# Windowed attention with a soft mixture of experts on one core: the attention stage looped over pairs of head groups instead of single groups

## Chip, cores and metric

One NeuronCore of a Trainium2 chip runs the whole program. The metric is the device time of one execution in microseconds (us), as the median of several runs. PE is the matrix engine (PEld its weight loads), DVE the vector engine, ACT the scalar engine, POOL the GpSimd engine, SP the engine whose queue issues nearly all DMA transfers. Each engine works through its own instructions in program order, and semaphores make it wait for others.

## What is computed

```python
# q, k, v: (8 batches, 8 heads, 576 positions, 64)
scores = (q @ k^T) / 8 + bias           # bias = -slope[head] * |i - j|
scores = where(0 <= i - j < 128, scores, -1e9)
attn   = exp(scores - max); attn /= sum + 1e-9
x      = (attn @ v) as (4608 tokens, 512)
logits = x @ phi                        # 8 experts x 4 slots = 32 columns
d = softmax of logits over all tokens;  c = softmax of logits over the 32 slots
slot_input = d^T @ x                    # (8, 4, 512)
slot_out   = relu(slot_input @ w1[e]) @ w2[e]
out        = c @ slot_out               # (4608, 512)
```

## The kernel before, in words

**Tiles and groups.** A batch has five query tiles: t = 0 to 3 with 128 queries and t = 4 with 64. A query sees 128 keys back, so a tile's keys lie in its own and the previous tile. The eight heads of a tile are done as two groups g = 0, 1 of four heads (tile 4 has one group for all eight). `groups` (line 150) lists all 72 groups (b, t, g); the last batch takes its tiles in the order 1, 2, 3, 4, 0.

**The steps of a group.**
- `scores` (225): matmuls into one of two score buffers `s4s[i % 2]` in PSUM: a bias by a ramp (L231, L243, bf16), then q times k (L236, L250). The array is split into tiles of 64 rows by 32 columns there.
- `softmax_front` (306), for the new group and the one before it (`old`): on DVE `merge` (L263 to L267) lays the two halves of the window over each other, `rowmax` (L281) takes the maximum, `inverse` (L293) the reciprocal of the old group's sums, `bias` (L284) the new group's scaled maximum, `normalise` (L298) multiplies the old group's four blocks by the reciprocals. Between merge and maximum in the program, `total` (L289) adds an epsilon to the old group's sums, on POOL. `filler` puts pending small DVE steps of the slot softmax between them.
- `expo` (327): four exps on ACT (L333) with their row sums; they read the score buffer and write P into one of three buffers `p4s`.
- `flip` (338): four transposes of P on PE (L343) into the PSUM bank `pt`; full 128x128 layout.
- `split` (345): ACT copies the flipped P to SBUF (L350); in tiles 1 to 3 two selects on POOL cut it into the part that belongs to the previous tile's keys (L352) and the part of the own tile's keys (L354); tile 4 has its own pair (L357, L359). Tile 0 has no previous keys and needs no select.
- `values` (364): P times v on PE (L380) into the PSUM bank `xp`, in tiles of 128 rows by 64 columns. Both selects must be done, since each pair of heads uses both parts.
- `x_store` (389): when both groups of a tile are done, ACT copies the result from `xp` (L396).

**What happens to x.** Per batch: `x_flip` (398, L401) transposes each tile into the bank `xq`, `x_keep` (409, L410) copies it on ACT; `logits` (415, L419; every second batch also the packed tail tiles, L430) multiply x by phi into the bank `mi`; `token_*`, `slot_*` and `slots_*` do a running softmax over tokens and one over slots, with small transposes (L458, L486), `slot_sum` (498, L502; with a tail L509) and an update of the accumulator on DVE (`slot_add`, L515).

**PSUM.** Eight banks: two score buffers of two banks each, and one bank each for `pt`, `xp`, `xq`, `mi`. A bank is written again only when its reader has finished.

**The order of work.** The order on each engine is the order of the program (`manual_schedule` over all five). The loop (773 to 800) runs over groups i: softmax front of group i, flip and split of group i - 3 (`FLAG`), values of group i - 4 (`LAG`), scores of group i + 1, loads, exps of group i. Steps on x are put into lists by `do` in `after_values` (726) and taken out by `run` at five places of an iteration. `load_weights_at` (716) issues weight loads in between, some 36 of them during attention. Behind the loop stand the last groups and the joining of the slot statistics, written out by hand (802 to 889), and then the experts and the output (891 on).

Of the kernel before, what the change touches and what calls it, by code (L numbers as in the profile page):

```python
# [21 lines left out]
DM = H * D  # L22
# [22 lines left out]
LAG = 4  # L45
# [22 lines left out]
def tile_attn_softmoe(  # L68
# [55 lines left out]
    place = [ks[1], areas[14], ks[0], ks[2]] + [areas[i] for i in (0, 10, 6, 4, 16, 12, 8)]  # L124
# [273 lines left out]
    def x_flip(b, t, to=None):  # L398
        xq = ps_1.tile([P, DM], F32, tag="xq", name="xq") if to is None else to
        for j in range(NPAIR):  # L400
            nc.tensor.transpose(xq[:, P * j:P * j + P], x_of(b, t)[:, j], ident)  # L401
        st["xq", b, t] = xq
# [95 lines left out]
    def slot_sum(b):  # L498
        dn = st["d", b]
        ap = ps_1.tile([P, DM], F32, tag="mi" if b < last else "pt", name="ap")  # L500
        for c in range(lanes(b)):
            nc.tensor.matmul(  # L502
                ap[NS * c:NS * c + NS], lhsT=dn[:, NS * c:NS * c + NS], rhs=xns[c],
                start=True, stop=(c < 3 or not with_tail(b)),
            )
        st["a", b] = ap
# [209 lines left out]
    def load_weights_at(i):  # L716
        b, t, g = groups[i]
        if i >= W0 and loaded[0] < NW and (NW - loaded[0]) * (WEND - W0 - 2) >= NW * (WEND - i):
            load_weight()
        if groups[i] == (last, 3, 1):  # L720
            load_v(True)
        if b == last and (t == 0 and g == 0 or t == 4):
            assert loaded[0] >= NW
            load_weight()

    def after_values(i, key):
        b, t, g = key
        if not (g == 1 or t == 4):
# [6 lines left out]
        x_store(b, t, nc.scalar)  # L735
        tail = with_tail(b)
        late = b > 0 and b % 2 == 0
        if p == 0 and late:
            do("mid", i + 3, x_flip, b, t)
            do("act", i + 4, x_keep, b, t)  # L740
        elif t < 4:
            do("pe", i + 1 + (p == 1 and late), x_flip, b, t)
            if b < last or p == 0:
                do("act", i + 2 + (p == 0 or p == 1 and late), x_keep, b, t)
        if p == (4 if b < last else 1):
            do("pe", i + 1, logits, b)
            if tail:
                do("pe", i + 1, logits_tail, b)
            if b == last:
                return  # L750
            do("act", i + 2, token_copy, b)
            do("dve", i + 2, token_max, b)
            do("pe", i + 2, slot_flip, b)
            do("act", i + 3, token_exp, b)
            do("dve", i + 3, token_sum, b)
            do("pe", i + 3, token_flip, b)
            do("act", i + 4, token_keep, b)
            do("pre", i + 4, slots_max, b)
            do("pe", i + 4, slot_sum, b)
            do("act", i + 5, slots_exp, b)  # L760
            if tail:
                do("pe", i + 2, x_flip, b, 4)
                do("pe", i + 4, x_keep, b, 4)
                do("pe", i + 5, slot_tail, b)
                do("dve", i + 5, slot_add, b)
            else:
                do("pre", i + 5, slot_add, b)
            do("dve", i + 6, later, slots_norm, b)

    with tc.manual_schedule(engines=ORDERED):  # L770
        scores(0)
        loads(0)
        for i in range(n):
            new = groups[i]
            run("pre", i)
# [28 lines left out]
        def bank(tag):  # L804
            return ps_1.tile([P, NPAIR, P], F32, tag=tag, name="bank")

        def quarters(x):
            return x.rearrange("p (u w) -> p u w", u=4)

        x_keep(last, 2)  # L810
        token_copy(last)
# [3 lines left out]
        slot_flip(last)  # L815
        token_max(last)
        values(ga)
        load_weight()
        load_weight()
# [3 lines left out]
        flip(gc, to=quarters(free[0]))  # L823
        split(gc)
        token_exp(last)
        total(gd, LO)
        inverse(gd, LO)
        normalise(gd, LO)
        values(gb, range(0, 2), bank("xq"))
        flip(gd, LO)  # L830
        split(gd, LO)
        total(gd, HI)
        inverse(gd, HI)
        normalise(gd, HI)
        values(gb, range(2, 4))
        load_weight()
        flip(gd, HI, quarters(free[2]))
        split(gd, HI)
        token_sum(last)
        x_store(last, 3)  # L840
# [47 lines left out]
        run("dve", n)  # L888
# [225 lines left out]
```

## Time and profile before

| | |
|---|---|
| median of 3 runs | 297.35 us (297.21 to 297.76) |
| profiled execution, own time | 297.64 us |
| its span, first to last instruction | 295.9 us |
| mean granted PE clock | 0.974 |
| PE busy / weight loads | 277.5 / 196.7 us |
| DVE, ACT, POOL busy | 240.8, 208.6, 93.2 us |
| attention loop | to about 220 us |

The timeline of a view gives the start of an instruction (or of a run of equal ones) in us from the span's start, its length, the engine, the line, what it writes and reads, its shape and the count; in brackets how long the engine stood idle before it and whose event ended that. A flip counts as four PE records, values of a group of tiles 1 to 3 as 16, scores as 8 of the bias and 32 of q times k. Matmuls overlap, and their ends are modelled, so distances between starts tell more than lengths. [...]

### The profile page before, as it was taken

To read this page: it belongs to the slowest core of one execution; us is meant where nothing else is said; L and a number is where in the kernel's file an instruction comes from. 1 tells how busy PE (TensorE), PEld (TensorE's weight loads), DVE (VectorE), ACT (ScalarE), POOL (GpSimd) and SP (SyncE) were. 2 spreads that over 40 slices of the span, in tenths; PEclk is the share of its full clock that TensorE was granted. 3 is DMA by queue.
4 is the path that set the end of the run, shared out by engine and by line. 5 is a ranking of instruction groups with operands and counts; after the bars stand their busy time and mean duration, and the time that the engine had idled before them with its cause. 6 is when DMAs were issued, how large, how long until landed. Compare 5 with 4: busy or idle time off the path is not lost. (4 is left out here: it accounts for less than half of the span.)

```text
span 295.9 us, 13063 instructions
## 1 busy us (share of the span) xinstructions
PE 277.5 (94%) x5131; PEld 196.7 (66%) x5131; DVE 240.8 (81%) x745; ACT 208.6 (70%) x814; POOL 93.2 (31%) x207
## 2 busy tenths in 40 slices
PE   5599999999999999999999999999898999999990
PEld 2367877777677777776777777667676653587650
DVE  2899999998989999988999998979897345646451
ACT  3688888977988988977888977978686331035460
POOL 2025525442444254244415442445454011000000
PEclk9579999999999999999999999999999999999996
DMA  6545268878686878867688877857357489999897
GB/s 203 187 130 174 78 200 255 274 234 259 200 255 219 259 245 276 265 204 249 207 275 260 278 233 240 255 182 234 110 167 281 144 292 327 411 409 342 336 384 278
DMA packets 36753, 72.58 MB, mean 245 GB/s; under 512 B 4402, under 2 KB 15316, under 8 KB 36692
## 3 DMA queue, kind: packets, MB, share of 16 engines
q1 hardware_dynamic: 35972, 71.24, 72.7%
q8 instruction: 40, 0.66, 0.9%
q10 hardware_dynamic: 720, 0.51, 0.5%
q14 instruction: 21, 0.17, 0.2%
HBM read 62.29 MB, written 9.44 MB: 242 GB/s over the span
## 5 line engine op out<-in xcount | busy, mean ns | idle before, releaser
L333 ACT ACTIVATE area<-s,nb 128x128 f32<-128x128 f32 x288 | 102.7, 377 | 17.3 <-DVE nb L284 13.0
L380 PE MATMUL xp<-area 128*64 128x128 f32 (+1 forms) x1104 | 78.1, 273 | 1.7 <-DMA area<-v_n 0.9
L298 DVE TENSOR_SCALAR area<-area,rs 128x128 f32<-128x128 f32 x286 | 79.0, 337 | 0.4
L380 PEld LDWEIGHTS xp<-area 128*64 128x64 f32 (+1 forms) x1104 | 58.1, 136 | 17.7 <-issue 9.9
L333 ACT ACTIVATION_READ_ACCUMULATOR area<-s,nb 128x1 f32 x288 | 61.8, 214 | 0.0
L281 DVE TENSOR_REDUCE s<-s 128x4 f32<-128x512 f32 (+1 forms) x73 | 50.4, 690 | 2.3
L350 ACT COPY area<-pt 128x512 f32<-128x512 f32 (+1 forms) x72 | 42.3, 590 | 13.3 <-PE pt L343 12.2
L289 POOL TENSOR_SCALAR rs<-sm 128x4 f32<-128x4 f32 x70 | 14.1, 202 | 100.8 <-ACT area L333 100.0
L343 PE MATMUL pt<-unit_r,area 128*128 128x128 f32 x282 | 45.4, 284 | 0.0
L250 PE MATMUL s<-kq 64*32 64x160 f32 x1792 | 42.6, 305 | 0.0
L343 PEld LDWEIGHTS pt<-unit_r,area 128*128 128x128 f32 x282 | 31.8, 143 | 14.1 <-PE s L250 5.0
L352 POOL TENSOR_SCALAR_AFFINE_SELECT area<-area 128x512 f32<-128x512 f32 x48 | 31.3, 651 | 27.1 <-ACT area L350 25.4
L265 DVE COPY_PREDICATED s<-cst,s 128x512 f32<-128x512 int32 x48 | 33.0, 686 | 1.0 <-PE s L250 0.8
L354 POOL TENSOR_SCALAR_AFFINE_SELECT area<-area 128x512 f32<-128x512 f32 x48 | 31.4, 655 | 3.3
L250 PEld LDWEIGHTS s<-kq 64*32 64x32 f32 x1792 | 29.9, 108 | 0.7
L396 ACT COPY area<-xp 128x512 f32<-128x512 f32 (+1 forms) x37 | 20.7, 560 | 5.5 <-PE xp L380 5.3
L243 PE MATMUL s<-ramp,ones 64*32 64x320 bf16 x448 | 18.9, 314 | 5.5 <-ACT area L333 5.4
L401 PE MATMUL xq<-unit_r,area 128*128 128x128 f32 x136 | 22.1, 285 | 0.8 <-ACT area L410 0.7
L410 ACT COPY area<-xq 128x512 f32<-128x512 f32 x34 | 20.6, 605 | 0.2 <-PE xq L401 0.2
L401 PEld LDWEIGHTS xq<-unit_r,area 128*128 128x128 f32 x136 | 14.4, 140 | 7.4 <-issue 3.9
L985 ACT COPY ob<-po 128x512 f32<-128x512 f32 x19 | 10.4, 591 | 11.4 <-PE po L983 9.7
L243 PEld LDWEIGHTS <-ones 64*32 64x32 bf16 x448 | 7.1, 89 | 14.7 <-issue 7.2
(167 smaller groups left out, 330.7 us busy)
## 6 DMA issues: line engine op xcount, KB each, us to landing
w<-w SPq DMA_DIRECT2D x53, 512.0 KB, 5.0
out<-ob SPq DMA_DIRECT2D x36, 256.0 KB, 3.6
kq<-q_t SPq DMA_DIRECT2D x69, 128.0 KB, 3.1
kq<-k_t SPq DMA_DIRECT2D x32, 256.0 KB, 3.8
area<-v_n SPq DMA_DIRECT2D x31, 256.0 KB, 3.9
area<-w SPq DMA_DIRECT2D x8, 512.0 KB, 4.8
area<-v_n SPq DMA_DIRECT2D x12, 128.0 KB, 3.4
kq<-w SPq DMA_DIRECT2D x3, 512.0 KB, 5.3
```

Source lines behind the costliest of these rows:

```text
L243: nc.tensor.matmul(s4[32 * c:32 * c + 32, 2 * par:2 * par + 2, 32 * r:32 * r + WIN], lhsT=ones[rows, 0:32], rhs=ramp[rows, h], start=True, ...
L250: nc.tensor.matmul(s4[32 * c:32 * c + 32, 2 * par + jj, 32 * r:32 * r + WIN], lhsT=qt[rows, 2 * h + jj if t == 4 else jj, 32 * r:32 * r + 32],
L265: nc.vector.copy_predicated(s4[:, :, P:2 * P], bc(mask_u, 1, 4), s4[:, :, 0:P])
L281: nc.vector.tensor_reduce(st[key]["mx"][:, us], merged(key, us), axis=AX.X, op=ALU.max, negate=True)
L298: mul(p4[:, u], p4[:, u], st[key]["rs"][:, u:u + 1])
L333: nc.scalar.activation(s["p4"][:, u], merged(key, u), AF.Exp, bias=s["nb"][:, u:u + 1], scale=SCALE, accum_out=s["sm"][:, u:u + 1],)
L343: nc.tensor.transpose(s["pt"][:, u], s["p4"][:, u], ident)
L350: nc.scalar.copy(pa[:, us], s["pt"][:, us])
L352: nc.gpsimd.affine_select(pp[:, us], pa[:, us], [[0, m], [-1, P]], ALU.is_gt, 0.0, base=0, channel_multiplier=1)
L354: nc.gpsimd.affine_select(pa[:, us], pa[:, us], [[0, m], [1, P]], ALU.is_ge, 0.0, base=0, channel_multiplier=-1)
L380: nc.tensor.matmul(xp[D * par:D * par + D, j, 0:w], lhsT=v_slot[b, t - 1 + ph][0:rows, D * h:D * h + D], rhs=src[:, 2 * par + i] if t < 4 ...
L401: nc.tensor.transpose(xq[:, P * j:P * j + P], x_of(b, t)[:, j], ident)
```

## The change

The loop now runs over rounds, one per (batch, query tile), `rounds[:-2]`. A round r with the groups `keys` (two, or one for tile 4) does in this order: what is due in `front`; the softmax front of group i = first key + 3; flip and split of the first key; a flip of x of an earlier tile (and small flips of the slot work); flip and split of the second key, into the bank `xq`; logits if due; scores of group i + 1; exps of group i; small ACT steps; softmax front of group i + 1; values of both keys; scores of group i + 2; exps of group i + 1; the x store; small DVE steps. `LAG` is gone: values belong to the same round as the flips of their group.

The slot work of a batch b is spread by `slot_work` over the rounds that follow its tile 4: x flips of tiles 0 to 3 (and of the tail) one per round, logits in the next batch's tile 0, flips of the logits in tiles 1 and 2, the slot sum ahead of tile 3's round, a tail's slot sum ahead of tile 4's. In rounds of two groups the flip of x goes to the bank `xp`, which the values of the same round then use.

The code behind the loop changes with it: at its start all flips and values up to the fourth group from the end, and all scores, are issued in both versions; of the last three groups each step still stands there, in another order, and `slot_sum`, `slot_add` of the last batch but one and the x flips of two tiles of the last batch stand there too. Weight loads into freed areas start with three areas in `kq`, one of them ahead of the areas that came first.

```diff
-LAG = 4
...
-    place = [ks[1], areas[14], ks[0], ks[2]] + [areas[i] for i in (0, 10, 6, 4, 16, 12, 8)]
+    place = [ks[1], ks[0], ks[2]] + [areas[i] for i in (14, 0, 10, 6, 4, 16, 12, 8)]
...
-    def x_flip(b, t, to=None):
-        xq = ps_1.tile([P, DM], F32, tag="xq", name="xq") if to is None else to
+    def x_flip(b, t, to=None, tag="xq"):
+        xq = ps_1.tile([P, DM], F32, tag=tag, name="xq") if to is None else to
...
+    rounds = [[i for i in range(n) if groups[i][:2] == (b, t)] for b in range(B) for t in order(b)]
+
+    def slot_work(b):
+        r = 5 * b + 4
+        tail = with_tail(b)
+        for t in range(5 if tail else 4):
+            pair = t > 0 or b == last
+            do("flip", r + t, x_flip, b, t, None, "xp" if pair else "xq")
+            do("flip" if pair else "act", r + t, x_keep, b, t)
+        do("pe", r + 1, logits, b)
+        if tail:
+            do("pe", r + 1, logits_tail, b)
+        do("act", r + 1, token_copy, b)
+        do("dve", r + 1, token_max, b)
+        do("flip", r + 2, slot_flip, b)
+        do("act", r + 2, token_exp, b)
...
+        do("flip", r + 3, token_flip, b)
...
+        do("front", r + 4, slot_sum, b)
+        if tail:
+            do("front", r + 5, slot_tail, b)
+        do("mid", r + 4 + bool(tail), slot_add, b)
...
+    def next_scores(i):
+        if i < n:
+            scores(i)
+        if i < n - 1:
+            loads(i)
...
-            if i >= FLAG:
-                flip(groups[i - FLAG])
-                split(groups[i - FLAG])
-            run("act", i)
-            if i >= LAG:
-                values(groups[i - LAG])
-                after_values(i, groups[i - LAG])
-            if i + 1 < n:
-                scores(i + 1)
-            if i + 1 < n - 1:
-                loads(i + 1)
-            run("mid", i)
+            next_scores(i + 1)
             if i:
                 expo(new)
-            run("pe", i)
             load_weights_at(i)
-            run("dve", i)
+        for r, group in enumerate(rounds[:-2]):
+            keys = [groups[i] for i in group]
+            i = group[0] + FLAG
+            run("front", r)
+            softmax_front(groups[i], groups[i - 1])
+            flip(keys[0])
+            split(keys[0])
+            run("flip", r)
+            for key in keys[1:]:
+                flip(key, to=bank("xq"))
+                split(key)
+            run("pe", r)
+            next_scores(i + 1)
+            expo(groups[i])
+            run("act", r)
+            load_weights_at(i)
+            run("mid", r)
+            if len(keys) > 1:
+                softmax_front(groups[i + 1], groups[i])
+            for key in keys:
+                values(key)
+            after_values(*keys[0][:2])
+            if len(keys) > 1:
+                next_scores(i + 2)
+                expo(groups[i + 1])
+                load_weights_at(i + 1)
+            x_store(*keys[0][:2], nc.scalar)
+            run("dve", r)
...
```

More of the change, by code (lines that the diff above doesn't have):

```diff
@@ L499, in slot_sum @@
         dn = st["d", b]
-        ap = ps_1.tile([P, DM], F32, tag="mi" if b < last else "pt", name="ap")
+        tag = {last: "pt", last - 1: "xq"}.get(b, "mi")
+        ap = ps_1.tile([P, DM], F32, tag=tag, name="ap")
         for c in range(lanes(b)):
@@ L719, in load_weights_at, with after_values @@
             load_weight()
-        if groups[i] == (last, 3, 1):
+        if groups[i] == (last, 4, 0):
+            load_weight()
+        if groups[i] == (last, 0, 0):
+            assert loaded[0] > NW
             load_v(True)
-        if b == last and (t == 0 and g == 0 or t == 4):
-            assert loaded[0] >= NW
             load_weight()
-    def after_values(i, key):
-        b, t, g = key
-        if not (g == 1 or t == 4):
-            return
+            load_weight()
+    rounds = [[i for i in range(n) if groups[i][:2] == (b, t)] for b in range(B) for t in order(b)]
[13 more added lines that the diff above has]
+        do("act", r + 2, token_exp, b)
+        do("dve", r + 2, token_sum, b)
+        do("dve", r + 2, slots_max, b)
+        do("flip", r + 3, token_flip, b)
+        do("act", r + 3, token_keep, b)
+        do("act", r + 3, slots_exp, b)
+        do("dve", r + 3, later, slots_norm, b)
+        if b == last - 1:
+            return
+        do("front", r + 4, slot_sum, b)
+        if tail:
+            do("front", r + 5, slot_tail, b)
+        do("mid", r + 4 + bool(tail), slot_add, b)
+    def after_values(b, t):
         p = pos(b, t)
@@ L734, in after_values, with bank, quarters @@
             load_v()
[L735 to L768, printed above, removed]
+    for b in range(last):
+        slot_work(b)
+    def bank(tag):
+        return ps_1.tile([P, NPAIR, P], F32, tag=tag, name="bank")
+    def quarters(x):
+        return x.rearrange("p (u w) -> p u w", u=4)
+    def next_scores(i):
[3 more added lines that the diff above has]
+            loads(i)
     with tc.manual_schedule(engines=ORDERED):
@@ L772, in tile_attn_softmoe @@
         loads(0)
-        for i in range(n):
+        for i in range(FLAG):
             new = groups[i]
-            run("pre", i)
             if i:
@@ L783, in tile_attn_softmoe @@
                     expo(new, us)
-            if i >= FLAG:
-                flip(groups[i - FLAG])
-                split(groups[i - FLAG])
-            run("act", i)
-            if i >= LAG:
-                values(groups[i - LAG])
-                after_values(i, groups[i - LAG])
-            if i + 1 < n:
-                scores(i + 1)
-            if i + 1 < n - 1:
-                loads(i + 1)
-            run("mid", i)
+            next_scores(i + 1)
             if i:
                 expo(new)
-            run("pe", i)
             load_weights_at(i)
-            run("dve", i)
-        ga, gb, gc, gd = groups[n - 4:]
[L804 to L811, printed above, removed]
+        for r, group in enumerate(rounds[:-2]):
[26 more added lines that the diff above has]
+            run("dve", r)
+        ga, gb, gc, gd = groups[n - 4:]
         flip(gb)
@@ L814, in tile_attn_softmoe @@
         split(gb, HI)
[L815 to L819, printed above, removed]
+        logits(last)
+        flip(gc, to=quarters(free[0]))
+        split(gc)
+        token_copy(last)
+        total(gd, ALL)
+        inverse(gd, ALL)
+        normalise(gd, ALL)
+        slot_sum(last - 1)
         load_weight()
@@ L822, in tile_attn_softmoe @@
         nc.sync.dma_start(sel, seld[:, 0:2 * NS])
-        flip(gc, to=quarters(free[0]))
-        split(gc)
-        token_exp(last)
[L826 to L835, printed above, removed]
+        x_flip(last, 1, tag="xp")
+        x_keep(last, 1)
+        slot_add(last - 1)
+        slot_flip(last)
+        token_max(last)
+        flip(gd, to=quarters(free[2]))
+        split(gd)
+        values(gb, to=bank("pt"))
+        token_exp(last)
+        token_sum(last)
+        x_flip(last, 2)
+        x_keep(last, 2)
         load_weight()
[L837 to L840, printed above, removed]
+        load_weight()
         values(gc, to=quarters(free[0]))
```

1 line of the change is left out of this document (removed).

## Prediction

> **What bounds the kernel now.** I read the busy time in stretches first, then the timeline of PE, then those of the engines it exchanges data with. One stretch of the attention stage (busy us of PE, PEld, DVE, ACT, POOL; granted clock last but two):
>
> ```profile
> span 295.9 us, 13063 instructions
> 80.00:120.00 40.00, 39.55 (x752) 28.86 (x744) 38.13 (x122) 34.80 (x144) 16.84 (x35) 1.00 0.78 251
> ```
>
> PE works 39.55 of 40 us at the full clock. The profiled execution took 297.64 us, 0.29 above the median of 297.35; I sum against it and subtract that at the end. The PE timeline of one batch (start, length, line, tile, count) shows what the 40 us consist of:
>
> ```profile
> 96.05 0.66 PE L401 MATMUL xq<-unit_r,area 128*128 128x128 f32 x4
> 96.54 0.60 PE L343 MATMUL pt<-unit_r,area 128*128 128x128 f32 x4
> 97.07 0.66 PE L380 MATMUL xp<-area 128*64 128x128 f32 x8
> 97.66 0.33 PE L243 MATMUL s<-ramp,ones 64*32 64x320 bf16 x8
> 97.80 0.73 PE L250 MATMUL s<-kq 64*32 64x160 f32 x32
> 98.46 1.08 PE L419 MATMUL lp<-area,phi 128*32 128x128 f32 x32
> 99.47 0.66 PE L343 MATMUL pt<-unit_r,area 128*128 128x128 f32 x4
> ...
> 104.14 0.60 PE L401 MATMUL xq<-unit_r,area 128*128 128x128 f32 x4
> 104.58 0.60 PE L343 MATMUL pt<-unit_r,area 128*128 128x128 f32 x4
> 105.11 1.09 PE L380 MATMUL xp<-area 128*64 128x128 f32 x16
> 106.13 0.33 PE L243 MATMUL s<-ramp,ones 64*32 64x320 bf16 x8
> ...
> 106.93 1.07 PE L502 MATMUL ap<-area,dn 128*32 128x512 f32 x8
> 107.93 0.66 PE L343 MATMUL pt<-unit_r,area 128*128 128x128 f32 x4
> ...
> 119.34 2.31 PE L380 MATMUL xp<-area 128*64 128x64 f32 x32
> 121.58 0.33 PE L243 MATMUL s<-ramp,ones 64*32 64x320 bf16 x8
> ```
>
> From start to start: a flip behind a flip takes 0.44 (104.14 to 104.58), behind scores 0.49 (96.05 to 96.54), ahead of values 0.53 (96.54 to 97.07); values ahead of scores 1.02 (half of it in tile 0: 0.59; tile 4: 2.24); scores 0.80; logits 1.01; the slot sum 1.00. So each change of the array's layout (128x128, 128x64, 64x32) costs 0.05 to 0.15. That is what a PE without waits could save.
>
> **What each PE step feeds.** Behind a flip stand ACT's copy and two selects on POOL, and values wait for both selects. ACT and POOL, then DVE:
>
> ```profile
> 88.21 0.59 ACT L350 COPY area<-pt 128x512 f32<-128x512 f32 x1
> 88.88 0.64 POOL L352 TENSOR_SCALAR_AFFINE_SELECT area<-area 128x512 f32<-128x512 f32 x1 [0.27 <-ACT area L350]
> 89.58 0.64 POOL L354 TENSOR_SCALAR_AFFINE_SELECT area<-area 128x512 f32<-128x512 f32 x1
> 91.49 0.19 POOL L289 TENSOR_SCALAR rs<-sm 128x4 f32<-128x4 f32 x1 [1.27 <-ACT area L333]
> 91.75 0.62 ACT L410 COPY area<-xq 128x512 f32<-128x512 f32 x1
> 92.23 0.63 ACT L396 COPY area<-xp 128x512 f32<-128x512 f32 x1
> 92.81 0.37 ACT L333 ACTIVATE area<-s,nb 128x128 f32<-128x128 f32 x1
> 94.20 0.60 ACT L350 COPY area<-pt 128x512 f32<-128x512 f32 x1
> 97.25 0.59 ACT L350 COPY area<-pt 128x512 f32<-128x512 f32 x1
> ```
>
> ```profile
> 90.32 0.86 DVE L298 TENSOR_SCALAR area<-area,rs 128x128 f32<-128x128 f32 x4
> 91.11 0.68 DVE L265 COPY_PREDICATED s<-cst,s 128x512 f32<-128x512 int32 x1
> 91.82 0.70 DVE L281 TENSOR_REDUCE s<-s 128x4 f32<-128x512 f32 x1
> 92.43 0.17 DVE L293 RECIPROCAL rs<-rs 128x4 f32<-128x4 f32 x1
> 92.55 0.16 DVE L284 TENSOR_SCALAR nb<-s 128x4 f32<-128x4 f32 x1
> 92.70 1.31 DVE L298 TENSOR_SCALAR area<-area,rs 128x128 f32<-128x128 f32 x4
> ```
>
> Flip to copy is 0.71 (96.54 to 97.25), copy to second select's end 2.01 (88.21 to 90.22). Before, values of a group stand behind the next group's flip, 2.93 (96.54 to 99.47) or 3.35 us (104.58 to 107.93) later: that work of PE covered the 2.7 us.
>
> **The change, part by part.** PE in a masked round (tiles 1 to 3), before and after; L343/L342 are flips of P, L401/L400 of x, L458/L457 a flip of the logits, L380/L379 values, L250/L249 scores:
>
> ```order
> L458 MATMUL dp<-unit_r,lg 128x128
> L343 MATMUL pt<-unit_r,area 128x128 x4
> L380 MATMUL xp<-area 64x128 x8
> ...
> L250 MATMUL s_0_82<-kq 32x160 x16
> L486 MATMUL dp<-unit_r,lg 128x128
> L401 MATMUL xq<-unit_r,area 128x128 x4
> L343 MATMUL pt<-unit_r,area 128x128 x4
> L380 MATMUL xp<-area 64x128 x8
> ```
>
> The same round after:
>
> ```order
> L342 MATMUL pt<-unit_r,area 128x128 x4
> L400 MATMUL xq<-unit_r,area 128x128 x4
> L457 MATMUL dp<-unit_r,lg 128x128
> L342 MATMUL bank<-unit_r,area 128x128 x4
> ...
> L249 MATMUL s_1_83<-kq 32x160 x16
> L379 MATMUL xp<-area 64x128 x16
> ...
> L249 MATMUL s_0_82<-kq 32x160 x16
> ```
>
> Six layout changes become four, and values now follow the flips of the same group, with one scores group between. POOL in two such rounds, before and after:
>
> ```order
> L289 TENSOR_SCALAR rs<-sm 128x4
> L352 AFFINE_SELECT area<-area 128x512
> L354 AFFINE_SELECT area<-area 128x512
> L289 TENSOR_SCALAR rs<-sm 128x4
> L352 AFFINE_SELECT area<-area 128x512
> L354 AFFINE_SELECT area<-area 128x512
> ```
>
> After, L288 is `total`, L351 and L353 the selects:
>
> ```order
> L288 TENSOR_SCALAR rs<-sm 128x4 x2
> L351 AFFINE_SELECT area<-area 128x512
> L353 AFFINE_SELECT area<-area 128x512
> L351 AFFINE_SELECT area<-area 128x512
> L353 AFFINE_SELECT area<-area 128x512
> L288 TENSOR_SCALAR rs<-sm 128x4 x2
> ```
>
> The sums' `total` of the round's first softmax now stands behind all four selects. ACT around two groups before, and in one masked round after (pt and bank: flipped P; xq: flipped x):
>
> ```order
> L333 ACTIVATE area,sm<-s_0_82,nb 128x128 x4
> L350 COPY area<-pt 128x512
> L333 ACTIVATE area,sm<-s_1_83,nb 128x128 x4
> L350 COPY area<-pt 128x512
> L410 COPY area<-xq 128x512
> L396 COPY area<-xp 128x512
> ```
>
> After:
>
> ```order
> L349 COPY area<-pt 128x512
> L409 COPY area<-xq 128x512
> L349 COPY area<-bank 128x512
> L332 ACTIVATE area,sm<-s_0_82,nb 128x128 x4
> L494 COPY dn<-dp 128x128
> L530 ACTIVATE ln<-ln 128x128
> L332 ACTIVATE area,sm<-s_1_83,nb 128x128 x4
> L395 COPY area<-xp 128x512
> ```
>
> The x store (L395) stands behind the second four exps, the next round's first copy behind the store, and on PE the x flip waits for it too (they share a bank), with the second flip and the scores queued behind.
>
> *PE alone.* A pair took 0.80+0.49+0.53+1.02 and, without a flip of x, 0.80+0.58+1.02 (0.58 is 0.49+0.53-0.44), 5.24 us; it takes 0.80+0.49+0.44+0.53+0.80+0.92+0.96, 4.94 us (the values' 1.02 less 0.1 for leaving the layout, or less 0.06 for entering it). That is -0.30, in 31 pairs -9.3.
>
> *Two chains around a masked round*, from the start of the copy of its first flip. Common part: 0.67 to the first select (88.21 to 88.88), three times 0.70 and 0.64 for four selects: they end at 3.41. Chain A, over PE: hop 0.08 (88.80 to 88.88), values of the second group 1.02, scores 0.80, flip to copy 0.71: 6.02. Chain B, over program order: hop 0.08, `total` 0.19, hop 0.08, reciprocal 0.12, bias 0.16, hop 0.10 (92.71 to 92.81), four exps of the second softmax 1.39 (92.81 to 94.20), x store 0.48 (the pitch of copies, 91.75 to 92.23): 6.01. Both close on the next round's first copy, so a masked round can't be shorter than 6.0, whatever PE saves. On DVE bias and normalises are queued behind the reciprocal that waits, and the exps wait for the bias. Four normalises fall into the selects: beside a select they took 1.31 (92.70) against 0.86, and the select can lose some too, between 0 and 0.2 us per round; I take 0.1: **6.1**. The four end about 2.4, behind the second select, so that the second softmax's merge and maximum (0.71 and 0.61 by the DVE rows) are done at 3.7, with `total`. PE then idles some 1.1 us per round. The Trainium skill's page "SBUF — State Buffer" (Who interferes with whom) says that a VectorE operation in a 2-port mode and a GpSimd operation lock each other out for a whole instruction; the 1.31 agrees. By it alone every normalise could wait out a select.
>
> Two more rows for the other rounds, the logits with those of a tail tile (PE), and the update of the accumulator (count, shortest, median, longest ns):
>
> ```profile
> 69.51 1.08 PE L419 MATMUL lp<-area,phi 128*32 128x128 f32 x32
> 71.39 0.66 PE L343 MATMUL pt<-unit_r,area 128*128 128x128 f32 x4
> ```
>
> ```profile
> L515 DVE SCALAR_TENSOR_TENSOR acc<-acc,al,ap x5: 740/748/748, 84.4 to 195.2; 128x512 f32<-128x512 f32 x5
> ```
>
> *The other rounds.* Tile 0 has no selects, but scores wait for x flip, second flip and logits, and the x flip for the x store that frees its bank: 0.25+0.44+0.53+1.01 = 2.23 (0.25: the store, 0.63 long, starts 0.48 ahead of the first copy, and a hop), then scores to their end 0.87 (97.66 to 98.53) and a hop 0.1, merge 0.71, maximum 0.61, reciprocal and bias 0.28, hop 0.1, exps 1.39, x store 0.48: **6.8**, and with a tail tile's logits (1.88, 69.51 to 71.39) **7.7**. Tile 4: 0.67, two selects 1.34, hop 0.08, values 2.24, flip to copy 0.71: **5.05**. The slot sum stands between scores and flip ahead of tile 3's round: +1.0 on chain A of tile 2's, **7.05**. With a tail the tail's slot sum, taken at the same 1.0, does so ahead of tile 4's: **7.05** for tile 3's; without one the accumulator's update on DVE (0.75) stands ahead of the second softmax there, of which 0.1 is spare on chain B: **6.7**.
>
> The flips at which batch 0 (from its tile 1), batches 1 to 6 and the last batch's two rounds begin, and where these end:
>
> ```profile
> 18.94 0.66 PE L343 MATMUL pt<-unit_r,area 128*128 128x128 f32 x4
> 37.28 0.66 PE L343 MATMUL pt<-unit_r,area 128*128 128x128 f32 x4
> 203.17 0.66 PE L343 MATMUL pt<-unit_r,area 128*128 128x128 f32 x4
> 217.12 0.60 PE L343 MATMUL pt<-unit_r,area 128*128 128x128 f32 x4
> ```
>
> *The sum.* Batch 0 from its tile 1: 3 x 6.1 + 5.05 = 23.35, before 18.34. Batches 1 to 6: three of 6.8+6.1+7.05+6.7+5.05 = 31.7 and three of 7.7+6.1+7.05+7.05+5.05 = 32.95, together 193.95, before 165.89. Last batch: logits fall into a masked round, 6.8, and 6.1, 12.9, before 13.95. Together 230.2 against 198.2: **+32.0**. The changed tail behind it holds the same operations; I take it and the weight loads that SP now issues a little earlier as 0, and +-2 for it. 297.64 + 32.0 - 0.29 = **329.4 us** (rounded up).
>
> **Rivals.** (1) Faster, 5%: PE stays the bound and saves its 9.3 us, 288.0. It needs values to find their selects done. From flip to second values PE has 0.49+0.44+0.53+0.80+0.92 = 3.18 us of work, the data needs 0.71+3.41+0.08 = 4.20; each select would have to take 0.45 instead of 0.70 (at 0.52 the change comes out even). POOL's rows, all at 0.64 to 0.66, speak against it; PE's 99% speaks for it. [...] (2) Only chain A holds, because the x store or `total` doesn't delay what follows: masked rounds 6.02, tile 0 as PE's sum, 5.15 or 6.0. Batches 29.25 and 31.1, batch 0 23.1, last 12.0: 216.2, +18.0, 315.3; 13%. (3) Each select blocks one normalise, so that the second softmax starts behind the fourth select instead of the second: +1.2 in 23 masked rounds, 357; 6%. (4) The gains in PE and the stalls cancel (select chains partly overlap in a way that I miss): about 297, 2%.
>
> **How the numbers follow.** The forecast has 74%: 329.4, its own range 320 to 340 (0.1 in the masked rounds' hops and locks is 2.3 us, 0.3 in each of the other 13 rounds 3.9, the tail 2). The range that holds 8 in 10 takes in rival 2: 314 to 343. A measurement of this kernel can tell 0.2% from no change: faster 0.06, same 0.01, slower 0.93.
>
> **What would show it.** In the profile after, PE's busy share in the attention stage should fall to about 0.85 or lower, masked rounds should repeat every 6.0 to 6.3 us, values should wait for POOL's second and fourth select (some 0.5 us each), and DVE's reciprocal for POOL's `total`. If values start without such a wait, and PE stays at 99%, the forecast is wrong; if the waits are there and rounds last 5.3, only the first chain's size is.

## The result and the profile after

The changed kernel takes **330.98 us** (median of four executions, 327.18 to 332.11) against 297.56 for the kernel before (297.21 to 299.79): 1.107 times as long, with an interval of 1.102 to 1.112. The ratios here and below are of undisturbed executions alone, so this one lies a little under the quotient of the two medians, 1.112. The forecast was 329.4, with a range of 314 to 343.

The profiled execution took 327.18 us. First the page's span and its row of busy times, then the stretch of the attention stage that was shown of before (busy us of PE, PEld, DVE, ACT, POOL; granted clock last but two):

```profile
span 325.5 us, 12985 instructions
PE 279.9 (86%) x5131; PEld 197.6 (61%) x5131; DVE 241.2 (74%) x742; ACT 210.9 (65%) x814; POOL 95.7 (29%) x207
...
80.00:120.00 40.00, 34.71 (x711) 25.10 (x714) 34.39 (x107) 29.82 (x121) 14.61 (x31) 1.00 0.67 208
```

Every engine has about the work it had before (PE 279.9 us against 277.5, DVE 241.2 against 240.8), but in 40 us PE now does 34.71 us of it instead of 39.55. The array waits. The table of waits (engine and line, what released it, us in total, times, longest) names for whom:

```profile
ACT area L332 <- DVE nb L283: 36.0, 30, 3.2
DVE s L264 <- PE s L249: 29.4, 20, 4.4
PE xq L400 <- ACT area L395: 13.3, 14, 1.5
PE xp L379 <- POOL area L353: 8.8, 26, 0.7
DVE rs L292 <- POOL rs L288: 3.6, 8, 0.8
```

The last two wait on POOL: the values (L379) for a group's second select (L353), 26 times, and the reciprocal (L292) for `total`, 8 times only. The x flip (L400) waits for the x store (L395) that frees its bank. The first two show engines handing work to each other in turn: the exps wait for DVE, DVE for the scores, and PE stands still in between.

One masked round, tile 1 of batch 3, from one first-flip copy to the next, on the engines that take part (start, length; in brackets the idle time before and what ended it):

```profile
115.30 0.62 ACT L349 COPY area<-pt 128x512 f32<-128x512 f32 x1
115.49 0.66 PE L400 MATMUL xq<-unit_r,area 128*128 128x128 f32 x4 [1.50 <-ACT area L395]
...
116.09 0.60 PE L342 MATMUL bank<-unit_r,area 128*128 128x128 f32 x4
...
116.62 0.33 PE L242 MATMUL s<-ramp,ones 64*32 64x320 bf16 x8
116.64 1.70 DVE L297 TENSOR_SCALAR area<-area,rs 128x128 f32<-128x128 f32 x4 [0.35 <-DVE nb L283]
116.70 0.72 POOL L353 TENSOR_SCALAR_AFFINE_SELECT area<-area 128x512 f32<-128x512 f32 x1
...
117.42 1.31 PE L379 MATMUL xp<-area 128*64 128x128 f32 x20
...
118.26 0.68 DVE L264 COPY_PREDICATED s<-cst,s 128x512 f32<-128x512 int32 x1
...
118.89 0.88 PE L379 MATMUL xp<-area 128*64 128x128 f32 x12 [0.15 <-POOL area L353]
118.92 0.19 POOL L288 TENSOR_SCALAR rs<-sm 128x4 f32<-128x4 f32 x1
118.98 0.70 DVE L280 TENSOR_REDUCE s<-s 128x4 f32<-128x512 f32 x1
119.59 0.17 DVE L292 RECIPROCAL rs<-rs 128x4 f32<-128x4 f32 x1
...
119.99 0.37 ACT L332 ACTIVATE area<-s,nb 128x128 f32<-128x128 f32 x1 [0.65 <-DVE nb L283]
...
121.38 0.60 ACT L395 COPY area<-xp 128x512 f32<-128x512 f32 x1
...
121.84 0.62 ACT L349 COPY area<-pt 128x512 f32<-128x512 f32 x1
```

The round takes 6.54 us (115.30 to 121.84). Follow it back from its end: the copy at 121.84 stands behind the store (121.38), the store behind four exps (119.99 on), these behind the second softmax on DVE, whose merge starts at 118.26. The scores that it merges are done by about 117.6 (an estimate: a round without selects, shown below, merges 1.01 us behind the start of its scores, here 116.62). But the four normalises (L297, 116.64), beside the selects, take 1.70 us and hold DVE until 118.34. `total` (118.92) is done at 119.11, and the reciprocal starts at 119.59, when the maximum is through. So `total` isn't what DVE waits for here.

### The profile page after: what moved, and what is told of

Read it like the earlier page. It is cut to its first block, busy times and chain, and to the rows that moved or that the text cites. A ratio compares the mean times of both kernels' runs of the same rounds, so it can differ in the third digit from the quotient of the medians.

```text
span 325.5 us, 12985 instructions
## 1 busy us (share of the span) xinstructions
PE 279.9 (86%) x5131; PEld 197.6 (61%) x5131; DVE 241.2 (74%) x742; ACT 210.9 (65%) x814; POOL 95.7 (29%) x207
## 5 line engine op out<-in xcount | busy, mean ns | idle before, releaser
L379 PE MATMUL xp<-area 128*64 128x128 f32 (+1 forms) x1104 | 77.7, 273 | 17.5 <-POOL area L353 8.8
L297 DVE TENSOR_SCALAR area<-area,rs 128x128 f32<-128x128 f32 x286 | 81.2, 346 | 1.7 <-DVE nb L283 0.3
L379 PEld LDWEIGHTS xp<-area 128*64 128x64 f32 (+1 forms) x1104 | 57.7, 136 | 38.6 <-POOL area L353 18.8
L332 ACT ACTIVATION_READ_ACCUMULATOR area<-s,nb 128x1 f32 x288 | 60.5, 210 | 0.0
L264 DVE COPY_PREDICATED s<-cst,s 128x512 f32<-128x512 int32 x48 | 33.1, 689 | 29.6 <-PE s L249 29.4
L351 POOL TENSOR_SCALAR_AFFINE_SELECT area<-area 128x512 f32<-128x512 f32 x48 | 31.0, 646 | 25.9 <-ACT area L349 21.0
L353 POOL TENSOR_SCALAR_AFFINE_SELECT area<-area 128x512 f32<-128x512 f32 x48 | 34.5, 719 | 3.3
L400 PE MATMUL xq<-unit_r,area 128*128 128x128 f32 x136 | 22.0, 285 | 13.3 <-ACT area L395 13.3
L349 ACT COPY area<-pt 128x512 f32<-128x512 f32 (+1 forms) x40 | 23.6, 595 | 8.1 <-PE pt L342 8.1
L395 ACT COPY area<-xp 128x512 f32<-128x512 f32 (+1 forms) x38 | 21.1, 556 | 9.2 <-PE xp L379 9.2
L400 PEld LDWEIGHTS xq<-unit_r,area 128*128 128x128 f32 x136 | 14.8, 141 | 19.2 <-ACT area L395 16.6
L342 PE MATMUL pt<-unit_r,area 128*128 128x128 f32 x156 | 26.0, 290 | 0.0
L342 PEld LDWEIGHTS pt<-unit_r,area 128*128 128x128 f32 x156 | 16.6, 142 | 13.7 <-DVE s L262 4.2
L349 ACT COPY area<-bank 128x512 f32<-128x512 f32 x31 | 18.4, 592 | 2.9 <-PE bank L342 2.6
L342 PE MATMUL bank<-unit_r,area 128*128 128x128 f32 x124 | 20.0, 286 | 0.0
```

Of the source, the lines that this page charges most:

```text
L264: nc.vector.copy_predicated(s4[:, :, P:2 * P], bc(mask_u, 1, 4), s4[:, :, 0:P])
L297: mul(p4[:, u], p4[:, u], st[key]["rs"][:, u:u + 1])
L332: nc.scalar.activation(s["p4"][:, u], merged(key, u), AF.Exp, bias=s["nb"][:, u:u + 1], scale=SCALE, accum_out=s["sm"][:, u:u + 1],)
L342: nc.tensor.transpose(s["pt"][:, u], s["p4"][:, u], ident)
L349: nc.scalar.copy(pa[:, us], s["pt"][:, us])
L351: nc.gpsimd.affine_select(pp[:, us], pa[:, us], [[0, m], [-1, P]], ALU.is_gt, 0.0, base=0, channel_multiplier=1)
```

## The experiments

Twelve kernels in all. Each is given against the kernel before in the same set of runs (medians of 297.8 to 298.5 there).

**Which wait? Three edits to the changed kernel.** The first leaves the selects where they are, but lets them write tiles that nobody reads, so that the values use the uncut P:

```diff
-                pa[:, us], pa[:, us], [[0, m], [1, P]], ALU.is_ge, 0.0, base=0, channel_multiplier=-1)
+                pp[:, us], pa[:, us], [[0, m], [1, P]], ALU.is_ge, 0.0, base=0, channel_multiplier=-1)
...
-        s.update(pd=pa, pp=pp)
+        s.update(pd=pa, pp=pa)
```

> The changed kernel, with both selects of a group writing into a tile that nobody reads, and values reading the unmasked copy for both parts (so the window's cut between own and previous keys is left out). POOL does the same work at the same place; only the wait of the values for the selects is gone. Theory A (values stand still until the selects are done, and that sets the round): masked rounds fall from 6.1-6.5 us to PE's own 5.0-5.3, 23 of them, so 305 to 312 us. Theory B (the round is set by DVE's normalises, which the selects block, then the second softmax, its exps, the x store and the next round's first copy, all in program order): masked rounds stay within 0.2 us, 326 to 332 us.

Measured: 317.8 us (ratio 1.063, 1.057 to 1.069), 13 us less than the change, between the two theories. Its profile in the round of tile 1 of batch 3, and one line of the next round:

```profile
109.98 1.70 DVE L297 TENSOR_SCALAR area<-area,rs 128x128 f32<-128x128 f32 x4 [0.34 <-DVE nb L283]
...
110.76 1.97 PE L379 MATMUL xp<-area 128*64 128x128 f32 x32
...
112.93 0.17 DVE L292 RECIPROCAL rs<-rs 128x4 f32<-128x4 f32 x1
...
119.07 0.18 DVE L292 RECIPROCAL rs<-rs 128x4 f32<-128x4 f32 x1 [0.41 <-POOL rs L288]
```

The values (L379) now run in one piece without a wait, and still the rounds from tile 1 to tile 2 of the first four batches take 5.97, 6.35, 6.31 and 6.54 us, where the changed kernel takes 5.96, 6.35, 6.31 and 6.54. What got shorter are above all the rounds of tile 4, from 4.7 to 3.5, then those of tile 2, which hold a slot sum, from 6.73 to 7.32 down to 6.44 to 6.91, and some of tile 3 (6.34 instead of 7.08 in batch 2). So the wait of the values adds to these, as the first chain of the forecast has it, but it does not set the rounds of tile 1. In tile 1's round the reciprocal doesn't wait for `total`; in the next, of tile 2, it does (0.41).

The second puts the x store ahead of the second exps, to cut the chain of the round shown at its end:

```diff
+            x_store(*keys[0][:2], nc.scalar)
             if len(keys) > 1:
                 next_scores(i + 2)
                 expo(groups[i + 1])
                 load_weights_at(i + 1)
-            x_store(*keys[0][:2], nc.scalar)
```

> The changed kernel with one line moved: ACT's x store stands ahead of the second group's four exps instead of behind them, nothing is left out. Theory B: the store (0.48 us of ACT) leaves the chain in every pair round: tile 0's rounds lose 0.4 to 0.5, masked rounds lose it until the values' wait for the selects binds at about 5.9, so 0.2 to 0.4: 318 to 323 us. Theory A (the selects alone): only tile 0's rounds gain, 326 to 329 us.

Measured: 331.73 us (1.111, 1.108 to 1.115): no gain, and slower than either theory had it. Its profile, in tile 1's round of batch 3:

```profile
118.65 0.70 POOL L353 TENSOR_SCALAR_AFFINE_SELECT area<-area 128x512 f32<-128x512 f32 x1
...
119.41 0.88 PE L379 MATMUL xp<-area 128*64 128x128 f32 x12 [0.29 <-POOL area L353]
...
120.33 0.59 ACT L395 COPY area<-xp 128x512 f32<-128x512 f32 x1 [0.72 <-PE xp L379]
...
121.06 0.37 ACT L332 ACTIVATE area<-s,nb 128x128 f32<-128x128 f32 x1
```

The store now waits for the second values, and these for the fourth select. The exps behind the store start 5.10 us behind the round's first copy (115.96), later than in the changed kernel (4.69, 115.30 to 119.99), so that the store has left the chain at its end and the exps end it later. The rounds from tile 1 to tile 2 take 6.23, 6.27, 6.46 and 6.49 in the first four batches: one chain for another. Tile 0's round, which holds no select, does gain what was expected (6.87 instead of 7.36 in batch 2).

The third moves the normalises behind the second softmax's bias, away from the selects:

```diff
-        normalise(old, HI if first else ALL)
+        if not late:
+            normalise(old, HI if first else ALL)
...
-                softmax_front(groups[i + 1], groups[i])
+                softmax_front(groups[i + 1], groups[i], True)
+                normalise(groups[i - 1], ALL)
+                normalise(groups[i], ALL)
```

> The changed kernel with the normalises of both softmax fronts of a pair round issued behind the second front's bias, so that no normalise stands between the first and the second softmax while POOL selects. Nothing is left out. Theory B with the blocked normalises as the delay: the second softmax starts 0.5 us earlier in masked rounds; `total` behind the selects and the values' wait then bind at 5.9 to 6.0: 0.3 us less in 23 rounds, 321 to 326 us. If the blocked normalises don't matter: within 2 us of the changed kernel.

Measured: 331.28 us (1.111, 1.107 to 1.115), no gain over all. In the round of the same place:

```profile
117.28 0.70 DVE L264 COPY_PREDICATED s<-cst,s 128x512 f32<-128x512 int32 x1 [0.69 <-PE s L249]
...
118.82 1.65 DVE L297 TENSOR_SCALAR area<-area,rs 128x128 f32<-128x128 f32 x8
...
120.03 0.42 PEld L343 LDWEIGHTS pt<-unit_r,area 128*128 128x128 f32 x4 [0.25 <-DVE area L297]
```

The merge now waits for the scores only, and the eight normalises, free of the selects, take 1.65 us, less than the four beside them did. The rounds from tile 1 to tile 2 gain in the odd batches: 5.99 instead of 6.35 in batch 1, 5.98 instead of 6.54 in batch 3, 5.99 instead of 6.07 in batch 5. In batches 2 and 4 they stay at 6.31. It is given back at other places: tile 3's rounds take 6.43 and 7.37 instead of 6.27 and 7.08 (the first flip, L343, now waits for normalises), and three rounds of tile 4 and three of tile 0 are longer (5.34 to 5.45 instead of 4.7, and 8.15, 8.16 and 8.57 instead of 7.35), because PE's clock fell there (the last section). Four such falls lengthen this profile's rounds by some 6 us, against 1.56 for the one in the changed kernel's; less these, an estimate, the loop takes 224.5 here and 224.9 there. So the gain of tile 1's rounds is nearly all lost to the other rounds, and the clock hides little more. The normalises do set tile 1's rounds in the odd batches, by 0.1 to 0.6 us.

With the normalises out of the way another wait comes forward. In this run's table of waits

```profile
DVE rs L292 <- POOL rs L288: 14.2, 18, 1.4
```

the reciprocal waits for `total`, behind the selects, 18 times instead of 8.

**Both causes, crossed.** The next edit takes the selects out of the changed kernel (the cut is left out), and out of the kernel before as a control:

```diff
-        if 0 < t < 4:
-            nc.gpsimd.affine_select(
...
-        s.update(pd=pa, pp=pp)
+        s.update(pd=pa, pp=pa)
```

> The changed kernel without any select on POOL (values read the unmasked copy for both parts; the window's cut is left out). Theory B keeps a chain without selects: x store, x flip (same bank), second flip, scores, second softmax, exps, x store, as in tile 0's rounds without the logits: 5.5 to 5.75 us in masked rounds, 311 to 319 us. If the selects are all that holds the rounds: PE's 5.0 to 5.3, 300 to 306 us.

> Control: the kernel before without any select on POOL (values read the unmasked copy; the window's cut is left out). If the kernel before is bound by PE and its selects are fully covered, nothing changes: 297 to 298.5 us. If the selects cost it something too (blocked normalises on DVE), it falls by up to 3 us. The no-select version of the changed kernel (305.9) is then to be held against this one.

Measured: 305.92 us (1.025, 1.021 to 1.028) without selects in the changed kernel, and 294.39 (0.987, 0.984 to 0.989) in the one before. Even with no selects the changed order is 11.5 us behind. Its time lies in the range given for selects that are all that holds the rounds (300 to 306), but only the masked rounds of its first batch, which flip no x, repeat every 5.02 us; those of the later batches take 5.4 to 6.9. One of them, of 5.98 us from x flip to x flip:

```profile
104.05 0.66 PE L389 MATMUL xq<-unit_r,area 128*128 128x128 f32 x4 [1.49 <-ACT area L384]
...
104.65 0.60 PE L342 MATMUL bank<-unit_r,area 128*128 128x128 f32 x4
...
105.18 0.33 PE L242 MATMUL s<-ramp,ones 64*32 64x320 bf16 x8
...
106.19 0.70 DVE L264 COPY_PREDICATED s<-cst,s 128x512 f32<-128x512 int32 x1
...
107.99 0.37 ACT L332 ACTIVATE area<-s,nb 128x128 f32<-128x128 f32 x1
...
109.38 0.60 ACT L384 COPY area<-xp 128x512 f32<-128x512 f32 x1
...
110.03 0.66 PE L389 MATMUL xq<-unit_r,area 128*128 128x128 f32 x4 [0.69 <-ACT area L384]
```

This is a loop that holds no select: the x flip waits for the store (L384 in this kernel), the second flip and the scores stand behind the x flip (1.13), the second softmax behind the scores (2.81 to its exps), the store behind the exps (1.39), the next x flip behind the store (0.65). Together 5.98. In the changed kernel the same loop is 6.54 long, and the difference lies where DVE is held by the normalises: from the scores to the merge 1.64 (116.62 to 118.26) instead of 1.01 (105.18 to 106.19). In batches 2, 4 and 6 tile 1's round takes 6.31 with selects and without, and tile 0's rounds, with the logits in this loop, keep their 6.49 and 7.35: there it is enough by itself.

If that loop and the selects are two causes, each enough by itself, then the store moved ahead must gain nothing with selects, as it did, and much without. The edits of e2 and e4 together:

> The changed kernel without its causal selects (the cut is left out, as in e4: 305.9 us) and with the store of x ahead of the second exps (as in e2, which gained nothing while the selects were there). Values in the same round, 36 weight buffers, the tail as it was. Theory A (two chains, each enough by itself: the selects behind the copy, and the store of x behind the exps; only without both do the rounds of all batches take the 5.0 us that e4's first batch took): 290 to 298, no more than 294.4 (the kernel before without its selects) plus 1 per cent, and masked rounds from 5.0 to 5.5. Theory B (the store behind the second values is as late as behind the second exps, selects or not): 303 to 308.

Measured: **292.66 us** (0.983, 0.979 to 0.986). First the stretch of the kernel before without its selects, then that of this one, then this one's first-flip copies of four rounds:

```profile
80.00:120.00 40.00, 39.99 (x804) 29.75 (x800) 35.35 (x126) 34.65 (x143) 2.53 (x13) 1.00 0.81 250
```

```profile
80.00:120.00 40.00, 38.42 (x754) 29.00 (x750) 35.34 (x127) 34.45 (x140) 2.79 (x14) 1.00 0.77 240
```

```profile
20.03 0.59 ACT L349 COPY area<-pt 128x512 f32<-128x512 f32 x1
24.91 0.60 ACT L349 COPY area<-pt 128x512 f32<-128x512 f32 x1
29.76 0.61 ACT L349 COPY area<-pt 128x512 f32<-128x512 f32 x1
34.54 0.59 ACT L349 COPY area<-pt 128x512 f32<-128x512 f32 x1
```

PE idles 1.58 of 40 us here, where before without selects it idles 0.01, and yet this kernel is no slower (292.66 against 294.39; the two intervals of the ratio overlap a little): PE's work did become less, as the forecast had it, and shows when little holds the values or the scores. Tile 1's round of batches 2, 4 and 6 is down from 6.31 to 5.62. The kernels in one table (us):

| | with selects | without |
|---|---|---|
| before | 297.56 | 294.39 |
| changed | 330.98 | 305.92 |
| changed, store first | 331.73 | 292.66 |

With selects the place of the store is worth nothing, without them 13.3 us. The selects cost 3.2 us before (4.1 within its own set of runs), 25.1 in the changed kernel, and 39.1 with the store first. Taking them out ends three things at once, though: the wait of the values, the lengthening of the normalises, and the place of `total` behind four selects. The first and the second were also taken away alone; no run took `total` off POOL, and none, with the values in their own round, put the store first with only one of the three gone.

**Can the order be kept and the waits be hidden?** The values of a round wait less if they are those of the round before. That needs four buffers for P and its cut instead of three and two, for which two of the 36 weight buffers go, and all work on x comes one round later:

```diff
-        i = number[key] % 2 if number[key] < n - 1 else 2
+        i = number[key] % 4
...
-            for key in keys:
+            for key in old:
                 values(key)
...
+            old = keys
```

> The changed kernel with the values of a round one round later (values of the previous tile stand where those of the own tile stood; four instead of two buffers for the masked P, 8 KB that come from two weight buffers fewer; slot work one round later). Nothing is left out. If the values' wait for the selects is one half of the loss and the x store behind the second exps (which x flip and next copy wait for) the other: masked rounds 5.5 to 6.0 us as in the version without selects, 304 to 313 us. If DVE behind the blocked normalises sets the rounds alone: 322 to 330 us.

Measured: 323.01 us (1.082, 1.076 to 1.087), not the 304 to 313 of the first guess, but in the range of the second. Its table of waits names another reason than the second guess does:

```profile
PE xq L402 <- ACT area L397: 19.2, 22, 2.6
```

The values' wait for POOL is down to a few times 0.3 to 0.5 us, and the x flip (L402) waits for the store (L397) more than before (13.3 us in the changed kernel). That is the loop seen without selects. So the next one also moves the store ahead of the second exps, where the values no longer hold it back, and another moves the normalises as well, as above:

> As the lagged version, and the x store ahead of the second exps (its values are now long done, so the exps shouldn't wait for it). Both halves of the loss are gone: rounds fall to what PE (4.94 and the slot work) or DVE (two softmax fronts, 5.0 in the rounds without flips of x and selects) leave, 5.1 to 5.5 us: 288 to 300 us. If the layout saving on PE isn't there, not below 297.

> As the lagged version with the store first, and both normalises of a pair round behind the second front's bias, away from the selects. If blocked normalises are what is late next: 1 to 4 us below the lagged version with the store first. If not: within 1 us of it, or some us above, since the flips of the next round wait for the later normalises.

Measured: 312.85 (1.049, 1.045 to 1.052) and 313.77 (1.051, 1.047 to 1.056): 10 us for the store, nothing for the normalises. The first was expected at 288 to 300, a clear miss. In its profile two rows stand out:

```profile
112.67 1.96 DVE L299 TENSOR_SCALAR area<-area,rs 128x128 f32<-128x128 f32 x4
...
117.47 0.33 PE L487 MATMUL dp<-unit_r,lg 128*128 128x128 f32 x1 [1.30 <-DVE ln L529]
```

Four normalises still take 1.96 us beside the selects, and a small flip (L487) waits for the work on the slots that DVE reaches late. The last runs take away each, and give up the two weight buffers in the kernel before, as a control:

```diff
-        do("dve", r + 2, slots_max, b)
+        do("mid", r + 2, slots_max, b)
```

> The kernel of e7 (values one round later, the store of x ahead of the second exps, 312.85 us) without the four causal selects of a round: the cut is left out, and the second copy of P is read as the first. Compare with the kernel before without its selects (294.4 us). Theory A (what is left in e7 is VectorE's normalises being blocked by the selects, some 0.3 to 0.6 us in each of 24 masked rounds, and the token flips behind slots_max): 312.85 less 7 to 14 us, 299 to 306. Theory B (once the chains are gone VectorE's own work of about 5.0 us a round and TensorE's of 4.94 leave no more than before had, so the layout saving of 0.30 us a pair at last shows): 285 to 292. Theory C (the flips of one round still stand behind a chain that holds no select): 309 or more.

> The kernel of e7 with the search for the slots' largest tokens on VectorE put ahead of that round's merges, rather than behind them, so that TensorE's flip of the tokens, which waited 7 times for about 1.2 us there, finds it done. Theory A (that wait is on the path): 312.85 less 4 to 8 us, 305 to 309, and the rounds from tile 1 to tile 2 go from 6.5 to about 5.5. Theory B (VectorE is the bound there, and moving its work only moves the wait to the scores): 311 to 314.

> Control: the kernel before with 34 weight buffers rather than 36, as the kernels with values one round later have. The loads of weights for the tail then start later. If that costs the tail, it shows here without any other edit: 297.4 plus 2 to 8 us, which would explain the longer tail of e7 (86 against 78 us from the last copy on). If not, 297 to 298.5, and the longer tail of e7 comes from the slot work that is one round later.

Measured: 299.73 without selects (1.005, 1.002 to 1.008); 313.43 with the early slots (1.053, 1.049 to 1.058), where the wait of the small flip is gone from the list, the values wait 4.9 us for a copy of x instead, and the time is the same; 300.11 for before with two buffers fewer (1.008, 1.006 to 1.010). So ending the small flip's wait gained nothing. The selects still cost 13.1 us in this order, though the values hardly wait for them any more. The groups of DVE's normalises, with the selects and without, show one way (busy us, mean ns of one):

```profile
L299 DVE TENSOR_SCALAR area<-area,rs 128x128 f32<-128x128 f32 x286 | 84.5, 358 | 0.8 <-issue 0.2
```

```profile
L299 DVE TENSOR_SCALAR area<-area,rs 128x128 f32<-128x128 f32 x286 | 62.6, 282 | 1.4 <-issue 0.2
```

The same 286 instructions take 21.9 us more beside selects. Before, they took 79.0 us too; there PE was the bound, and PE's weight loads waited for them 1.2 us in all. But this is not shown to be the way by which the 13.1 us are lost: the kernel with the normalises moved takes them in 60.1 us, as few as without selects, and gains nothing. In its table of waits

```profile
DVE rs L294 <- POOL rs L290: 12.8, 17, 1.4
```

the reciprocal waits for `total` 12.8 us (2.7 with the store first alone), and the weight loads of first flips wait 11.0 us for the normalises (4.3). When one way of the selects is closed, the next takes over; the share of each stays open.

From the first-flip copy of the first batch's tile 1 to that of the last batch's tile 3, the lagged kernel with the store first takes 205.9 us (20.49 to 226.34), without selects 192.5 (19.68 to 212.22), and the kernel before 198.1 (19.69 to 217.81). What follows takes 86.0, 87.4 and 78.1. The two buffers account for 2.7 of these 8 to 9 us (217.27 to 298.1 in their control, 80.8); the rest comes with what the lag pushes behind the loop, and was not tried apart. No version that keeps the selects beat the kernel before.

## Why the prediction was right

**The path to the number.** The loop was forecast 32.0 us longer, 230.2 against 198.2. It is 226.4 (20.97 to 247.38 by the copies' starts), 28.3 longer. The tail was taken at 0, and takes 78.1 in both. What wasn't in the sum: the first copy of tile 1 comes 1.3 later (20.97, before 19.69). Together 29.6, the difference of the spans. The median lies 3.8 us above the profiled execution, which goes with the clock (the last section) and is in no term of the sum, so the forecast is nearer to it than its terms deserve.

**By kinds of rounds.** Masked rounds were set at 6.1. They took 5.96, 6.00 and 6.37 in batch 0, and 6.07 to 6.54 from tile 1 to tile 2 of the later ones. Tile 0 was set at 6.8 and 7.7 and took 6.49 and 7.35: the sum let the x flip wait for the store, as in other rounds, but the round of tile 4 ahead of it stores half as much (0.37 us), and the flip starts 0.15 before the copy (108.67 and 108.82 in batch 3) instead of 0.25 behind it. Tile 4, set at 5.05, took 4.64 to 4.74: four of its 32 matmuls of values run behind the first select, ahead of the second. Tile 2's with the slot sum, set at 7.05, took 6.73 to 7.32; tile 3's, set at 6.7 and 7.05, 6.26 to 7.08.

**The layouts' saving** was right in kind: 31 pairs should save 0.30 each in PE, hidden behind the chains. Where the chains are gone it shows, but smaller: from tile 1 to tile 4 of batch 0 a pair takes 4.84 us without selects and with the store first (20.03 to 34.54), and 5.05 in the kernel before without its selects (19.77 to 34.93), 0.21 less. PE still idles in both: it is busy for 13.63 of those 14.51 us and for 14.80 of the 15.16 before, which is 0.39 less per pair. So the forecast 0.30 lies between the two readings.

**The step that failed** is the path of the second chain. The prediction had DVE's reciprocal wait for `total`, which stands behind four selects, and had the second softmax's merge and maximum done at 3.7 us, in time with `total`. By the trace the reciprocal waits so in 8 of 70 softmaxes, 3.6 us together. In most rounds two other things stand there. The loop over x flip, second flip, scores, second softmax, exps and store, which the sum used for tile 0 alone, also holds in rounds of tile 1 that flip x, at 5.98 or 6.31 without selects. And the normalises were given 0.1 us of loss and an end at about 2.4 us; beside the selects four of them take 1.70 instead of 0.87 and end 3.04 us into the round of batch 3, so that the merge moves from about 117.6 to 118.26. The wait for `total` is real, but mostly hidden behind these: it shows in the round of tile 1 of batch 0, which flips no x (the reciprocal waits 0.77 us there, and the round takes 5.96, with the values free 5.97), and it comes forward as soon as the normalises are moved. Of the signs that the prediction named, PE's share came (0.87), the plain masked rounds came or were longer (5.96 to 6.54), and the values' waits came (26 times, 0.34 on average); the reciprocal's did not in most rounds. That the sizes came out so near the sum's 6.1 is luck in so far as that loop, which the sum didn't have there, happens to be 5.98 long.

**The rivals.** PE as the bound (288) fell: PE is busy 34.71 of 40 us. Chain A alone (315.3) fell too: where no value waits for a select, tile 1's rounds stay as long as they were, and the time is still 317.8. The gains and stalls that cancel (297) fell with the result. The rival in which every select blocks a normalise (357) had the right mechanism for tile 1's rounds in the odd batches and too large a price, up to 0.56 us a round rather than 1.2 more than the forecast's 6.1: in the round of batch 3 two of the four normalises wait out a select (0.66 and 0.73 us long, the others 0.29 and 0.27). The Trainium skill's page "SBUF — State Buffer" (Who interferes with whom) says that a VectorE operation in a 2-port mode and one of GpSimd lock each other out for a whole instruction; the traces agree with a lock, with 1.65 us for eight normalises away from selects and 1.70 or 1.96 for four beside them, but not with one select per normalise. The Trainium skill's page "Perfetto Trace Analysis" (Identifying the Most-Contended Engine) would improve the engine with the highest occupancy first, but says that for TensorE the busy share of matmuls is not a good measure, and that of its weight loads is to be used beside the share of peak that it reaches. Here PE's matmuls were busy for 94% of the span before, its weight loads for 66% and DVE for 81%. The change cut PE's matmul work and is 10.7% slower; only without selects does the cut show, so the 94% alone didn't tell what it was worth.

## What to carry to other kernels

Before merging steps of a saturated engine to save its overheads, write down for each pair of steps what lies between producer and consumer on the other engines, and count the work of the saturated engine that covers it; here 3 us of it covered 2.7 us of copy and selects, and the new order left one scores group. Follow each loop of waits around a round to its end, through banks that must be freed and copies in program order too, for every kind of round: two loops of nearly the same length hide each other, so that removing one can show little or nothing. To find them, remove both, and then each alone, and look which wait comes forward.

## What was not expected of the hardware

The granted clock of PE fell to about half for one stretch of 3.4 us in the middle of attention, in kernels whose PE waits often. The stretch ahead of one, and the stretch itself, of the changed kernel:

```profile
40.60:44.00 3.40, 2.83 (x37) 2.10 (x38) 3.37 (x12) 2.14 (x10) 0.97 (x3) 1.00 0.47 136
44.10:47.50 3.40, 3.40 (x48) 2.57 (x50) 0.01 (x1) 2.84 (x10) 0.00 (x0) 0.51 0.27 77
```

PE had been busy for 2.83 of 3.40 us when the clock fell. The round in which it fell took 8.05 us, where the round of the same kind two batches later took 6.49: 1.56 us for one such stretch. The profile of before has none between 18 and 290 us, the three of changed orders without selects have none in the loop either, and that of the store ahead of the exps has five, one of them twice as long, with a mean clock of 0.951 (its 333.74 us less some 9 for them, an estimate, is 324 to 325, and the changed kernel's 327.18 less 1.56 is 325.6, so they hide no more than about 1 us of gain there). This goes with the spread of the changed kernel's executions: 327.18 us at a mean clock of 0.977, and 330.18 to 332.11 at 0.958 to 0.959, as far apart as two or three such stretches; the other executions have no trace that could show them. The Trainium skill's page "TensorE: Matmul & The Clock Gate" (HAM oscillation — how this bites in real kernels) ties such a fall to a whole window of idling; here the stretch ahead was 83% busy, and a stretch that was busy for only 60% (in the lagged kernel without selects) was not followed by one. What decides it stays open.
